# Moving three weight loads and shortening TensorE's last stretch in a fused attention and soft-MoE kernel

## The chip, the cores and the metric

The kernel runs on one core of one Trainium2 chip. The metric is device time in microseconds (us) of one execution, lower is better. A kernel's time is the median of its runs. A profiled execution gives the span, from the first instruction to the last, and a few microseconds lie around it.

## The reference: what is computed

Two layers follow each other. Shapes: batch 4, 8 heads, 768 positions, head size 64; the second layer sees 3072 rows of 512.

```python
# attention over the 6 best of 24 chunks of 32 keys
k_min, k_max = k_chunks.min(axis=3), k_chunks.max(axis=3)
ub = sum(maximum(q * k_min, q * k_max), axis=-1)       # bound per query and chunk
top_chunks = argsort(where(causal, ub, -1e9))[..., -6:]
scores = where(in_top_chunk & causal, q @ k.T / 8, -1e9)
attn_out = softmax(scores) @ v                         # -> x: [3072, 512]

# soft mixture of 8 experts with 4 slots each (32 slots)
logits = x @ phi                                       # phi: [512, 32]
d = softmax(logits, over the 3072 rows)
slot_input = d.T @ x                                   # [32, 512]
slot_out[e] = relu(slot_input[e] @ w1[e]) @ w2[e]      # w1: 512x1024, w2: 1024x512
c = softmax(logits, over the 32 slots)
out = c @ slot_out                                     # [3072, 512], float32
```

All inputs are float32 in memory. The loads turn them into bf16 on the way.

## The kernel before

**Pairs.** The attention works on 16 pairs of heads, four pairs per batch. For a pair i, `load` brings k and q (L146) and `load_v` brings v (L151). `transposes` (TensorE, L211) and `evac_T` (ScalarE, L220) turn k and q; `kmin`, `kmax` and `qsplit` (VectorE) and `ubound` (TensorE) make the bounds; `select` (VectorE's eight-largest operation, L274, and a copy of a flag on GpSimd, L276) finds the chunks; `ns_transposes` turns the resulting mask. `scores` (L303, L313) fills one of six groups of blocks, `expo` (ScalarE, L327) takes the exponential, `mask` (GpSimd, L337) clears the upper triangle of the diagonal blocks, `pv` (L355) multiplies by v, `normalise` (VectorE, L367, L368) divides, and `x_transposes` and `evac_x` turn the result for the second layer.

**Software pipeline.** All of this is written out by hand in one order; each engine executes its instructions in that order. In the loop, pass i takes the scores of pair i, the value product of pair i-1, the normalising of pair i-2, the turning of k and q of pair i+2 and the issue of the k and q loads of pair i+4. Every fourth pass also carries a step of the second layer for the batch that is done (`moe_...`): logits, a running maximum, the exponentials for dispatch and combine, and a dispatch product that is added to `si_acc`.

**Loads.** All loads are issued by GpSimd, in program order, on one queue. The loads use eight semaphores in turn, so that a load is not issued before the eighth load ahead of it has landed. The 16 expert matrices (w_sb, 1 MB each as bf16, L139) are `w_sb[0..7]` = w1 of experts 0 to 7 and `w_sb[8..15]` = w2 of experts 0 to 7. `load_w(0)` stands after the small phi load of the start; the other fifteen are spread over the passes by `wplan`, which says how many weights `weights(i)` issues in pass i: one each in passes 1 (as entry 0), 2, 3, 4, 5, 7, 8, 9, 10, 11, 12, 14 and 15, and two in 13. In passes below 14 they come after the k, q and v issues of the pass.

**The end.** After the loop, the last pair (LAST = 15) is finished: `pv(LAST, [0, 1, 2])`, `pv(LAST, [3])`, transposes and evacuation of pair 14, `pv(LAST, [4, 5])`, logits, transposes of pair 15, column sums of the combine weights (`col_sums`, L710), the last logits. Then come the maxima, the exponentials, the dispatch product (L491) and the experts. `keep(n)` issues n matmuls whose result nobody reads (L698). `experts_in` (L800) multiplies the slots by w1 in two halves of 512 hidden columns, four experts side by side, each in 32 columns of the array. `experts_out` (L838) does so with w2: experts 0 to 3 side by side, then experts 4, 5 and 6 side by side. Expert 7, whose w2 is loaded last, is cut by rows of its matrix into four parts that run side by side (`last_expert_out`, L849). Its four partial sums stand in spare rows of the result, and the combine weights `c_pad` of expert 7 are repeated four times (`spread_c`, L480) so that the last product adds them up. VectorE and ScalarE scale the result into `so_all` (L881 to L885), and the output stage multiplies it by the combine weights, scales it and stores it from the SyncE queue.

## Time and profile before

| what | value |
|---|---|
| median of 3 runs | 162.14 us (161.63 to 162.91) |
| profiled execution, whole | 162.55 us |
| its span | 160.8 us |
| TensorE (PE) matmul busy | 138.5 us, 86% of the span |
| VectorE (DVE) busy | 121.4 us, 75% |
| ScalarE (ACT) busy | 122.8 us, 76% |
| GpSimd (POOL) busy | 102.7 us, 64% |
| bytes moved by the DMA engines | 32.92 MB, mean 205 GB/s |

The page names an engine operation by the program's tiles and the line of the kernel. The line of digits cuts the span into 40 slices of 4.02 us, each digit being the busy share in tenths. The chain of waits follows the work that ended last back in time. In rows of the timeline, the first number is the start in us, the second how long the group lasted; a bracket tells how long the engine had been idle before it and who ended that. In the view of waits, the three numbers are the total in us, how many waits, and the longest. In the view by stretches of time, the columns after the length are the busy time of PE, PE's weight load (PEld), DVE, ACT and POOL, then PE's granted clock, the DMA share and GB/s. In the view of DMA issues, the last number is the time in us from issue to landing.

### The profile page before, as it was taken

Reading aid. Unit: us, or ns where it says so; the run is one execution under the profiler, and the core shown is the slowest. Engines: PE = TensorE matmul, PEld = TensorE weight load, DVE = VectorE, ACT = ScalarE, POOL = GpSimd, SP = SyncE. Lnnn points to the kernel's source line nnn. Section 1 sums busy time; section 2 is a strip of 40 time slices with the busy share of each in tenths; the row PEclk is TensorE's granted clock in tenths of the full one; section 3 lists DMA queues with packets and bytes.
Section 4 is the critical chain, followed back from the end, with each engine's and each line's share of the span. In section 5 each row is a group of like instructions: output and inputs, shape, how many; then the busy total and the mean of one; then the engine's idle time right before and its main releaser. Section 6 shows DMA issues by size and latency. Waiting matters only on the chain.

```text
span 160.8 us, 5896 instructions
## 1 busy us (share of the span) xinstructions
PE 138.5 (86%) x2420; PEld 91.7 (57%) x2420; DVE 121.4 (75%) x433; ACT 122.8 (76%) x169; POOL 102.7 (64%) x203
## 2 busy tenths in 40 slices
PE   7786799999999998999999899969899999987500
PEld 2343366766767686666768576646676854542100
DVE  4465989999999989998988899968862660187620
ACT  3679899999999898999989889968788521166520
POOL 7999577989888696988968986829864800000000
PEclk9999999999999999999999999999999999999965
DMA  3999999999999999999999999999999999329996
GB/s 40 141 120 158 206 197 206 201 182 211 194 210 196 209 200 206 198 182 211 197 210 195 214 191 212 195 207 197 209 203 214 213 217 213 67 71 415 419 419 248
DMA packets 40603, 32.92 MB, mean 205 GB/s; under 512 B 26368, under 2 KB 34816, under 8 KB 40576
## 3 DMA queue, kind: packets, MB, share of 16 engines
q0 software_dynamic: 38416, 26.25, 110.3%
q1 hardware_dynamic: 2160, 6.29, 9.7%
q8 instruction: 19, 0.31, 0.7%
q14 instruction: 8, 0.07, 0.1%
HBM read 52.49 MB, written 6.29 MB: 366 GB/s over the span
## 4 chain that ended last, share of the span: by engine, by line
PE 39%; DMA 23%; ACT 14%; DVE 11%; issue 5%; POOL 4%; DVEq 0%; ACTq 0%; POOLq 0%
DMA k_in<-in_k_dram 15%; ACT e_sb L327 8%; PE sc_ps L303 6%; PE at_ps L355 6%; DMA out_dram<-o_sb 5%; PE sc_ps L313 5%; PE tr_ps L211 4%; PE xT_ps L377 3%; DMA q_in<-in_q_dram 3%; ACT qT L220 3%; DVE mx L274 3%; PE h_ps L800 2%; PE so_ps L838 2%; DVE x_sb L368 2%; PE ub_ps L262 1%
## 5 line engine op out<-in xcount | busy, mean ns | idle before, releaser
L327 ACT ACTIVATE e_sb<-sc_ps 128x1024 bf16<-128x1024 f32 (+1 forms) x96 | 83.1, 917 | 7.1 <-PE sc_ps L313 6.5
L337 POOL TENSOR_SCALAR_AFFINE_SELECT e_sb<-e_sb 128x256 bf16<-128x256 bf16 x96 | 38.1, 414 | 18.5 <-ACT e_sb L327 18.0
L303 PE MATMUL sc_ps<-qT,kT 64*128 64x384 bf16 (+3 forms) x258 | 36.8, 305 | 2.5 <-ACT e_sb L327 1.6
L313 PE MATMUL sc_ps<-nsT,smask 64*128 64x384 bf16 (+2 forms) x294 | 38.1, 284 | 0.1
L355 PE MATMUL at_ps<-v_t,e_sb 128*128 128x65 bf16 x672 | 29.7, 194 | 1.9 <-DVE x_sb L368 1.5
L355 PEld LDWEIGHTS <-e_sb 128*128 128x128 bf16 x672 | 25.6, 98 | 4.1 <-issue 2.6
L274 DVE MAX8 mx<-ub_ps 128x8 f32<-128x8 f32 (+1 forms) x192 | 16.8, 162 | 4.2 <-PE ub_ps L262 4.2
L303 PEld LDWEIGHTS <-kT 64*128 64x128 bf16 x258 | 13.9, 93 | 10.7 <-issue 5.3
L313 PEld LDWEIGHTS <-smask 64*128 64x128 bf16 x294 | 14.9, 94 | 3.9 <-issue 0.6
L151 POOL DMA_DIRECT2D v_t<-in_v_dram x16 | 16.6, 1039 | 0.7 <-PE ns_ps L285 0.5
L229 DVE TENSOR_REDUCE mm<-kT 128x24 bf16<-128x768 bf16 x16 | 15.1, 945 | 2.3 <-ACT kT L220 2.3
L220 ACT COPY kT<-tr_ps 128x768 bf16<-128x768 bf16 x16 | 12.8, 802 | 4.8 <-PE tr_ps L211 4.8
L368 DVE TENSOR_TENSOR x_sb<-at_ps,inv 128x768 bf16<-128x768 f32 (+1 forms) x17 | 15.5, 910 | 0.6
L235 DVE TENSOR_REDUCE mm<-kT 128x24 bf16<-128x768 bf16 x16 | 15.1, 942 | 0.0
L220 ACT COPY qT<-tr_ps 128x768 bf16<-128x768 bf16 x16 | 12.8, 799 | 1.7 <-PE tr_ps L211 1.6
L146 POOL DMA_DIRECT2D k_in<-in_k_dram x16 | 11.7, 733 | 0.9 <-POOLq L930 0.8
L139 POOL DMA_DIRECT2D w_sb<-in_moe_w_dram x16 | 11.4, 711 | 0.9 <-DMA w_sb<-in_moe_w_dram 0.7
L146 POOL DMA_DIRECT2D q_in<-in_q_dram x16 | 11.5, 718 | 0.0
L211 PE MATMUL tr_ps<-ident,k_in 128*64 128x128 bf16 x192 | 8.4, 223 | 2.2 <-DMA k_in<-in_k_dram 1.7
L388 DVE COPY xT_sb<-xT_ps 128x768 bf16<-128x768 bf16 (+1 forms) x15 | 8.0, 536 | 2.6 <-PE xT_ps L377 2.6
L211 PE MATMUL tr_ps<-ident,q_in 128*64 128x128 bf16 x192 | 8.4, 223 | 0.8 <-DMA q_in<-in_q_dram 0.6
L377 PE MATMUL xT_ps<-ident,x_sb 128*128 128x128 bf16 x96 | 8.2, 221 | 0.0
(138 smaller groups left out, 202.7 us busy)
## 6 DMA issues: line engine op xcount, KB each, us to landing
w_sb<-in_moe_w_dram POOLq DMA_DIRECT2D x16, 1024.0 KB, 14.8
out_dram<-o_sb SPq DMA_DIRECT2D x10, 512.0 KB, 4.5
k_in<-in_k_dram POOLq DMA_DIRECT2D x16, 192.0 KB, 10.0
q_in<-in_q_dram POOLq DMA_DIRECT2D x16, 192.0 KB, 10.5
v_t<-in_v_dram POOLq DMA_DIRECT2D x16, 192.0 KB, 10.9
out_dram<-o_sb SPq DMA_DIRECT2D x2, 256.0 KB, 4.3
out_dram<-first SPq DMA_DIRECT2D x2, 128.0 KB, 2.0
out_dram<-first SPq DMA_DIRECT2D x1, 256.0 KB, 2.1
```

Of the source, the lines that this page charges most:

```text
L146: nc.gpsimd.dma_start(out=t, in_=src.rearrange("h (p g) d -> p h (g d)", p=P))
L151: nc.gpsimd.dma_start(out=v_t[i % NV][:, :, :, :D], in_=v[b, 2 * j:2 * j + 2].rearrange("h (g p) d -> p h g d", p=P),)
L211: nc.tensor.matmul(ps[h * 64:(h + 1) * 64, g, :], lhsT=src[:, h, g * D:(g + 1) * D], rhs=ident, is_transpose=True,)
L220: nc.scalar.copy(t.rearrange("d (p g) -> d p g", g=NQT), st.pop((nm + "ps", i)).rearrange("d g p -> d p g"),)
L229: nc.vector.tensor_reduce(mm[:, 0, 0, :], kT, axis=AX.X, op=ALU.min)
L274: nc.vector.max(mx[:, a, :], ub[:, a, :max(8, 4 * t + 4)])
L303: nc.tensor.matmul(ps[:, h, c:c + w], lhsT=kT[r, kg * P:(kg + 1) * P], rhs=qT[r, qs], start=True, stop=False,)
L313: nc.tensor.matmul(ps[:, h, c + (f - t0) * P:c + (l - t0) * P], lhsT=smask[r, x, kg].rearrange("p a b -> p (a b)"), rhs=nsT[r, (f - x * NJ ...
L327: nc.scalar.activation(e[:, :, :w], st.pop(("scps", i, g))[:, :, :w], func=ACT.Exp, scale=scale)
L337: nc.gpsimd.affine_select(out=e[:, :, c:c + P], in_=e[:, :, c:c + P], compare_op=ALU.is_ge, fill=0.0, base=0, pattern=[[0, 2], [1, P]], ch ...
L355: nc.tensor.matmul(o, lhsT=st["e", i, g][:, h, c:c + P], rhs=v_t[i % NV][:, h, kg, :], start=(kg == 0), stop=(kg == t),)
L368: nc.vector.tensor_tensor(st["x", b][:, t0:t1, 2 * j:2 * j + 2, :].rearrange("p t h d -> p h t d"), at[:, :, :, :D], inv.broadcast_to([P, ...
```

## The change

1. `load_w(0)` moves from behind phi to directly behind the q load of pair 1. The v load of pair 0 moves from before the first `select` to behind it.
2. In `wplan`, the weight of pass 5 moves to pass 6, and the weight of pass 10 joins that of pass 11. So w5 is issued after the k, q and v loads of pass 6 instead of before them, and w9 after those of pass 11.
3. In the last pair, the value products of query tiles 3, 4 and 5 share one accumulation and are ordered by the exponential group that feeds them: eight blocks (16 matmuls) before the transposes of pair 14, seven (14 matmuls) after. The column sums move ahead of the transposes of pair 15, and their reciprocal ahead of the last evacuation. The 18 logits of the first three quarters move behind these transposes.
4. The fillers after the dispatch product go from five to two.
5. The w2 matrices are loaded in the order of experts 0, 1, 2, 3, 5, 6, 7, 4. Expert 4 is now the one whose matrix is cut in four for the end. Experts 5, 6 and 7 are cut by rows into four equal shares of six steps, so that 24 matmuls run four side by side. The combine weights get a second repeated block to add the shares up: one of the three exponentials that fill `c_pad` becomes twice as wide, reads overlapping pairs of experts and needs one zeroed spare row in a fixed tile, `lc_sb`. The row of slot sums `zrow` gets one more small copy.

```diff
     load(1, "q")
+    load_w(0)
...
-    load_v(0)
     transposes(1, "q")
     evac_T(1, "q")
     spread_mask(NJ, NQT)
     select(0)
+    load_v(0)
     load_v(1)
...
     make_identity(nc, identf)
-    load_w(0)
     load(4, "k")
...
-    wplan = {0: 1, 2: 1, 3: 1, 4: 1, 5: 1, 7: 1, 8: 1, 9: 1, 10: 1, 11: 1, 12: 1, 13: 2, 14: 1, 15: 1}
+    wplan = {0: 1, 2: 1, 3: 1, 4: 1, 6: 1, 7: 1, 8: 1, 9: 1, 11: 2, 12: 1, 13: 2, 14: 1, 15: 1}
...
-    pv(LAST, [3])
-    at_b = st["at", LAST]
+    at_b = p_sc.tile([P, 2, 512], F32, name="at_ps", tag="sc")
+    def pv_last(blocks, start=False, stop=False):
...
+    pv_last([(3, 0), (3, 1), (3, 2), (4, 1), (4, 2), (4, 4), (5, 2), (5, 4)], start=True)
     x_transposes(LAST - 1)
     evac_x(LAST - 1, copy=nc.scalar.copy)
     normalise(LAST, 0, 3, at_a)
-    pv(LAST, [4, 5])
+    pv_last([(4, 3), (5, 1), (5, 3), (3, 3)])
+    pv_last([(4, 0), (5, 0), (5, 5)], stop=True)
...
-    moe_logits(BL, range(NDG - 1), lg12)
-    x_transposes(LAST, 0, 3)
-    evac_x(LAST, 0, 3, nc.scalar.copy)
-    normalise(LAST, 3, NQT, at_b)
-    x_transposes(LAST, 3, NQT)
-    evac_x(LAST, 3, NQT)
...
     for b in range(BL):
         col_sums(csa[:, b * NQT:(b + 1) * NQT], b)
+    x_transposes(LAST, 0, 3)
+    evac_x(LAST, 0, 3, nc.scalar.copy)
+    normalise(LAST, 3, NQT, at_b)
+    nc.vector.reciprocal(inv_a, csa)
+    x_transposes(LAST, 3, NQT)
+    evac_x(LAST, 3, NQT)
+    moe_logits(BL, range(NDG - 1), lg12)
     moe_logits(BL, range(NDG - 1, NDG), lg12)
...
     keep(2)
     moe_dispatch(BL)
-    keep(5)
+    keep(2)
...
+    def shared_out():
+        parts = [
+            [(5, x) for x in range(6)],
+            [(5, 6), (5, 7), (6, 0), (6, 1), (6, 2), (6, 3)],
+            [(6, 4), (6, 5), (6, 6), (6, 7), (7, 0), (7, 1)],
+            [(7, x) for x in range(2, 8)],
+        ]
+        for n in range(6):
+            for j in range(4):
+                e, fg = parts[j][n]
+                c0 = e * CH - (SPE if j == e - 5 else 0)
+                nc.tensor.matmul(
+                    so_ps[j * CH:(j + 1) * CH, :], lhsT=hT[:, fg, c0:c0 + CH],
+                    rhs=w_sb[E + LATE.index(e)][:, fg * Dm:(fg + 1) * Dm], start=False, stop=(n == 5),
+                )
...
-    experts_out([0], range(4))
+    experts_out(0)
     hidden_T(1)
     slot_sums()
-    experts_out([1], range(4))
-    experts_out([0, 1], [4, 5, 6])
+    experts_out(1)
+    shared_out()
```

More of the change, by code (lines that the diff above doesn't have):

```diff
@@ L99 @@
     c_pad = static.tile([P, NQT, 4, CH], BF16, name="c_pad")
+    lc_sb = static.tile([P, NQT + 1, NS], F32, name="lc_sb")
     si_acc = static.tile([P, NDG + 1, NS], F32, name="si_acc")
@@ L685 @@
     at_a = st["at", LAST]
-    pv(LAST, [3])
-    at_b = st["at", LAST]
+    at_b = p_sc.tile([P, 2, 512], F32, name="at_ps", tag="sc")
+    def pv_last(blocks, start=False, stop=False):
+        for n, (t, kg) in enumerate(blocks):
+            g, c = BLOCK_LAST[(kg, t)]
+            for h in range(2):
+                nc.tensor.matmul(
+                    at_b[:, h, (t - 3) * (D + 1):(t - 2) * (D + 1)],
+                    lhsT=st["e", LAST, g][:, h, c:c + P], rhs=v_t[LAST % NV][:, h, kg, :],
+                    start=(start and n == 0), stop=(stop and n == len(blocks) - 1),
+                )
+    pv_last([(3, 0), (3, 1), (3, 2), (4, 1), (4, 2), (4, 4), (5, 2), (5, 4)], start=True)
     x_transposes(LAST - 1)
@@ L720 @@
     tail = ctx.enter_context(tc.tile_pool(name="tail", bufs=1))
-    inv_a = tail.tile([P, BL * NQT], F32, name="inv_a")
-    nc.vector.reciprocal(inv_a, csa)
     m_old = m_run[(BL + 1) % 2]
```

60 lines of the change are left out of this document (29 added, 31 removed).

## The prediction

> **What bounds the kernel now.** I read the page, then the chain of waits, then the work by stretches of time, then single DMA issues with their time to landing, and last the timeline of the end.
>
> ```profile
> span 160.8 us, 5896 instructions
> DMA  3999999999999999999999999999999999329996
> PE 39%; DMA 23%; ACT 14%; DVE 11%; issue 5%; POOL 4%; DVEq 0%; ACTq 0%; POOLq 0%
> ```
>
> The DMA engines show 9 from the second slice to the 34th (about 4 to 137 us), while they load; the output follows. So there are two candidates for the start of the output stage: the loads, which move without a break, and the chain, most of which is PE. Both have to be followed to their meeting point.
>
> ```profile
> 118.63 0.77 POOL L139 DMA_DIRECT2D w_sb<-in_moe_w_dram  x1
> w_sb<-in_moe_w_dram POOLq DMA_DIRECT2D x1, 1024.0 KB, 21.5
> 140.21 0.28 PE L849 MATMUL so_last<-w_sb,hT_pad 128*32 128x256 bf16 x1
> 140.67 0.39 PE L849 MATMUL so_last<-w_sb,hT_pad 128*32 128x256 bf16 x6
> 140.89 0.49 DVE so_part L881
> 141.48 0.50 DVE so_all L883
> ```
>
> They meet here. The last weight is issued at 118.6 and lands 21.5 later, at 140.1; its first matmul starts at 140.21, on the landing. The other arm, PE's shared experts, lets DVE start so_part at 140.89, done at 141.38. Had PE been free, the eight so_last matmuls would end about 0.4 after the landing (six take 0.39 at 140.67), at 140.6, and so_all waits for so_part until 141.38. So today the compute arm is the later one, and the loads have only about 0.75 us of slack. A saving on one arm alone is worth little: compute alone at most 0.75, loads alone nothing.
>
> **The compute arm, part by part.**
>
> ```profile
> PE tr_ps L211 <- DMA k_in<-in_k_dram: 1.7, 2, 1.3
> 57.90 11.24 DMA k_in<-in_k_dram
> 93.29 12.66 DMA k_in<-in_k_dram
> ```
>
> *Two weights behind late k loads.* The chain passes through two k loads, those of pairs 10 and 15, and PE stood still for the two for 1.7 us in all (0.4 and 1.3). Each has a weight ahead of it in the queue. The change sends the k, q and v of pair 10 before w5, and those of pair 15 before w9, so each k lands earlier by one weight. A weight takes about 4.9 us (1,048,576 B at the 214 GB/s of the stretch from 18 to 22 us, shown below), far over 0.4 and 1.3. Both waits go; the loads behind the moved weight keep their place in the sum of bytes. What is late next: the chain is back on PE right after each wait, so I count the whole 1.7.
>
> ```profile
> 125.71 0.86 PE L355 MATMUL at_ps<-v_t,e_sb 128*128 128x65 bf16 x22
> 126.76 0.64 PE lgt_ps L400 x16
> 131.37 1.17 PE L698 MATMUL h_ps<-w_sb,ident 128*128 128x480 bf16 x5
> 131.63 0.35 DVE L773 TENSOR_TENSOR siT_pad<-si_acc,si_ps 128x64 bf16<-128x64 f32 x2 [0.38 <-PE si_ps L495]
> 132.48 2.77 PE L800 MATMUL h_ps<-w_sb,siT_pad 128*32 128x512 bf16 x48
> 136.57 0.86 PE so_ps L838 x16
> 138.09 2.31 PE so_ps L838 x34
> ```
>
> *Last pair.* After the transposes of pair 14, PE has 22 value matmuls in 0.86 (0.039 each) ahead of the second normalise. Eight of them now stand before the transposes, where DVE's normalise of pair 14 has PE waiting anyway, and 14 remain: 0.3 less. Against this, 18 logits (0.04 each by the row of 16, so 0.7) move behind the last transposes, into the time in which PE waited for the evacuation. If they overrun it, the 0.3 is gone. Between 0 and 0.3 I take 0.2. The column sums move ahead, into a wait for DVE; the reciprocal that reads them moves off the last logits into the same wait. I cost both at nothing.
>
> *Dispatch.* Five filler matmuls last from 131.37 to 132.54, and the experts start at 132.48, though siT_pad is written by 131.98. Three fillers fewer (0.2 each) take 0.6 away, but the experts still need siT_pad: start at 132.03, 0.45 less.
>
> *Experts.* With four experts side by side, 16 matmuls, four rounds, take 0.86: 0.215 a round. The shared three ran three side by side, 24 matmuls in eight rounds; now the same 24 run in six. Two rounds, 0.43. The row of 34 holds the second sixteen of the first four experts and most of the 24, and PE waits for nothing in it, so fewer rounds are less time.
>
> Sum of the compute arm: 1.7 + 0.2 + 0.45 + 0.43 = 2.8 us.
>
> *Costs at nothing.* In each batch one of three exponentials reads 192 elements instead of 96. An ACT row with 192 elements takes 0.33:
>
> ```profile
> 130.29 0.33 ACT L750 ACTIVATE d_sb<-lgt_ps 128x192 bf16<-128x192 f32 x1 [2.21 <-PE lgt_ps L741]
> ```
>
> so at most 0.33 is added per batch and 1.0 over the three inside the pairs, where ACT is nearly full; I take 0 because ACT's waits for PE in those pairs cover it, and keep the end for the range. At the end the ACT is idle until the first relu. The extra zrow copy is on a POOL that is empty by then.
>
> **The load arm.** Bytes do not change; only stretches in which the queue runs slowly can be won.
>
> ```profile
> 2.00:6.00 4.00, 3.41 (x21) 1.19 (x19) 0.95 (x13) 0.69 (x2) 3.83 (x10) 1.00 0.88 118
> 6.00:9.00 3.00, 2.48 (x40) 1.35 (x41) 2.38 (x4) 2.88 (x5) 3.00 (x5) 1.00 1.03 134
> 9.00:12.50 3.50, 3.14 (x42) 1.79 (x39) 2.67 (x16) 2.22 (x4) 3.32 (x6) 1.00 1.00 113
> 12.50:18.00 5.50, 3.37 (x50) 1.86 (x47) 3.80 (x19) 5.50 (x7) 4.71 (x11) 1.00 1.86 170
> 18.00:22.00 4.00, 3.56 (x69) 2.33 (x69) 3.35 (x18) 3.25 (x5) 2.21 (x5) 1.00 1.08 214
> 24.00:130.00 106.00, 100.53 (x1958) 72.62 (x1956) 92.51 (x327) 94.32 (x127) 82.72 (x162) 1.00 1.35 202
> ```
>
> The last column is GB/s. From 6 to 12.5 us the small loads crawl at 134 and 113, mean 123; later small loads alone reach 170, the first weight alone 214, the mixture 202. With w0 right behind the second q, the weight moves in that stretch. At 214 it takes 4.9 us; in 4.9 us the stretch moves 600 KB of small loads today, and these now follow at 170 (3.5 us) to 202 (3.0). The queue gains 4.9 − 3.5 = 1.4 to 4.9 − 3.0 = 1.9. If the weight crawls at 123 too, it gains nothing; with 214 for all, 2.1. I take 1.65, the middle of the two, since the rows nearest to it are this same weight and these same loads a few us later. The last weight then lands at 138.5.
>
> *What the moved weight pushes back.*
>
> ```profile
> q_in<-in_q_dram POOLq DMA_DIRECT2D x1, 192.0 KB, 4.3
> 4.75 0.74 POOL L146 DMA_DIRECT2D q_in<-in_q_dram  x1
> 12.81 0.72 POOL L139 DMA_DIRECT2D w_sb<-in_moe_w_dram  x1
> w_sb<-in_moe_w_dram POOLq DMA_DIRECT2D x1, 1024.0 KB, 10.6
> 13.52 0.72 POOL L146 DMA_DIRECT2D k_in<-in_k_dram  x1
> k_in<-in_k_dram POOLq DMA_DIRECT2D x1, 192.0 KB, 10.8
> 14.96 1.49 POOL L337 TENSOR_SCALAR_AFFINE_SELECT e_sb<-e_sb 128x256 bf16<-128x256 bf16 x4
> 15.95 0.53 PE L211 MATMUL tr_ps<-ident,k_in 128*64 128x128 bf16 x12
> 17.18 0.23 POOL L276 CAST ns_t<-mx 128x12 bf16<-128x12 f32 x1 [0.73 <-DVE mx L274]
> 21.31 0.55 PE L355 MATMUL at_ps<-v_t,e_sb 128*128 128x65 bf16 x12
> ```
>
> The second q lands at 4.75 + 4.3 = 9.1. Behind it w0 lands by 14.0, and a k or q takes about 1 us (w0 lands at 23.4, the k after it at 24.3): k of pair 2 at 15.0, needed at 15.95; its q at 16.0; v of pair 0, four loads and its own two us later, at 20, needed at 21.31. All in time, with about 1 us. On POOL the weight's issue (0.72) moves ahead of two masks and the loads of pairs 2 and 3, and the v issue (about 1 us) from before the first selection to behind it, so by that selection POOL has lost nothing. One new wait stands there: the loads take eight semaphores in turn, each load waits for the landing of the eighth before it, and in the changed order the q of pair 4 waits for the landing of pair 2's k. Behind it in POOL's queue stand four masks (1.49) and the flag copy that PE's next mask transposes need, at 17.18 today. 15.0 + 0.72 + 1.49 = 17.2: just in time. Up to 0.2 is possible; I take 0.
>
> **Where the arms meet.** Compute gains 2.8; the loads allow 0.75 + 1.65 = 2.4. The smaller counts: 2.4, so PE waits some 0.4 for the last weight. The output stage is not touched. The profiled execution took 162.55 us, span 160.8 plus 1.75 around it: 162.55 − 2.4 = 160.15, span 158.4. The execution lies 0.4 above the median of the runs, 162.14, which gives **159.7**.
>
> **The rivals.**
>
> *The first weight fills nothing.* Then the loads allow only today's 0.75: 162.14 − 0.75 = 161.4. For it: the slow stretch is one of small loads only, and if it belongs to them they are as slow behind the weight. The Trainium skill, DMA: Bandwidth & Descriptors, section Bandwidth, Measured, says it so: "Batch DMAs to ≥1 MiB for ≥75% of peak", with small transfers dominated by their descriptors; by it the 600 KB would still take 4.9 us and the gain be 0. Against it: 192 KB loads move at 170 from 12.5 us on, and the k behind w0 lands 0.9 us after it, over 200 GB/s; in that place the trace does not agree with the rule. 0.20.
>
> *The k waits only change their name.* PE is fed no faster because ACT or DVE, both nearly full in the pairs, end the next wait: compute gains 1.1 instead of 2.8, 162.14 − 1.1 = 161.0. Against it: the chain returns to PE after both waits. 0.12.
>
> *Slower: the start stalls.* If w0 crawls too, everything behind it is late. Each us past 14.0 at which w0 lands delays pair 2's k, the slot, the masks, the flag copy and so PE by one. At 113 GB/s w0 takes 9.3, lands at 18.4, 4.4 late; against 2.8 gained this is 1.6 lost: 163.7. It decides from 2.8 late, 16.8, which is 136 GB/s, about what the stretch moves today. Against it: packets of a weight ran at 214 beside the same work six us later. 0.08.
>
> **How the numbers follow.** Forecast 159.7 has 0.55: with loads at 1.4 to 2.1 and compute at 2.5 to 2.8 it spans 159.3 to 160.1. A better case, in which the last weight's straggling engines end closer together too (from 136 to 140.2 few of the 16 are busy) and compute keeps 2.8 to 3.5, 158.6 to 159.3, has 0.05. The range 158.8 to 161.4 leaves the slow start, half of the better case and the edge of the first rival out. A measurement tells about 1%, 1.6 us, from no change: faster takes the forecast, the better case and some tenth of the middle rivals, 0.65; same 0.30; slower, the tail of the slow start, 0.05.
>
> **What would show it.** In the profile after: no wait of PE for k near 69 and 106 us; w0 landing near 14 and 200 GB/s or more in the stretch from 8 to 13; pair 2's k before PE asks; the last weight landing near 138.5 with its first matmul right on it; shared experts in six rounds of 0.215; the experts' start right behind siT_pad. I am wrong if the GB/s of 6 to 13 stays near 123, if POOL's wait for the slot ends after 15 us, or if another wait replaces those for k.

## The result and the profile after

| | median us | runs | profiled execution | its span |
|---|---|---|---|---|
| before | 161.88 | 161.37 to 162.91 | 162.55 | 160.8 |
| after | 164.37 | 164.01 to 165.15 | 164.12 | 162.4 |

The changed kernel is slower: the ratio is 1.0145, with an interval of 1.0098 to 1.0192. The kernel before has one run more here than in the table ahead of the prediction, so its median is 161.88 instead of 162.14. The forecast was 159.7 us and its range ended at 161.4. In the kernel after, line numbers are 2 to 26 higher than in the kernel before; the tiles have the same names.

The page of the kernel after: its span, its DMA row and the shares of the chain.

```profile
span 162.4 us, 5892 instructions
DMA  3999999999999999999999999999999999329996
PE 30%; DMA 21%; DVE 19%; ACT 14%; POOL 6%; issue 5%; ACTq 0%; DVEq 0%; POOLq 0%; SPq 0%
```

PE's share of the chain fell from 39 to 30%. The shares alone do not say what took its place (that of DMA fell too, from 23 to 21%). The meeting point of the two arms, the loads and PE's own work, does: it is the last weight that ends last. In the view of DMA issues (last number: us from issue to landing)

```profile
w_sb<-in_moe_w_dram POOLq DMA_DIRECT2D x1, 1024.0 KB, 21.7
```

and in the timeline of GpSimd, PE and DVE:

```profile
119.89 0.77 POOL L141 DMA_DIRECT2D w_sb<-in_moe_w_dram  x1
...
139.44 1.47 PE L865 MATMUL so_ps<-w_sb,hT_pad 128*32 128x512 bf16 x24
140.97 0.48 DVE L907 TENSOR_SCALAR so_part<-so_ps,zinv 128x256 f32<-128x256 f32 x1 [2.17 <-PE so_ps L865]
141.67 0.40 PE L875 MATMUL so_last<-w_sb,hT_pad 128*32 128x256 bf16 x8 [0.76 <-DMA w_sb<-in_moe_w_dram]
142.65 0.60 PE L918 MATMUL oh_ps<-so_all,cT_all 128*128 128x256 bf16 x4 [0.37 <-DVE so_all L909]
```

The last weight lands at 119.89 + 21.7 = 141.6. Before it was 140.2, and the forecast had 138.5. PE now stands 0.76 us for it, which it did not do before. But PE's own arm is no earlier either: so_part is read at 140.97, against 140.89 before. The output begins at 142.65, which is 0.63 later than before (142.02), and the output stage then takes 19.77 us to the end of the span instead of 18.79. That makes 0.63 + 0.98 = 1.6 us, the difference of the two spans. (The profiles of two kernels below, e11 and e14, were taken in a disturbed execution and are not read.) There are three things to explain: where PE's saving went, why the last weight is late, and why a stage that the change does not touch is longer.

**PE's saving was made, and lost at the start.** The view of waits of the kernel after (us in all, times, longest):

```profile
PE tr_ps L215 <- DMA k_in<-in_k_dram: 0.8, 2, 0.6
```

The timeline of its dispatch:

```profile
132.70 0.35 DVE L782 TENSOR_TENSOR siT_pad<-si_acc,si_ps 128x64 bf16<-128x64 f32 x2 [0.31 <-PE si_ps L497]
132.98 2.77 PE L810 MATMUL h_ps<-w_sb,siT_pad 128*32 128x512 bf16 x48
```

The waits for k of pairs 10 and 15 are gone; 0.6 of the 0.8 us that is left is a new one at 16.92. The experts start 0.28 us after siT_pad begins to be written (before: 0.85). The 24 shared matmuls take 1.47 in one row. Measured between the same instructions, PE is 2.7 us late at k of pair 4 (30.02 against 27.29), 1.3 late at k of pair 15 (107.25 against 105.99), and 0.1 late at so_part. So passes (1.5), last pair (0.2), dispatch (0.57) and experts (0.42) returned some 2.65 us, and the start had taken 2.7.

**The start.** The view by stretches of the kernel after (last column GB/s, before it the DMA share and PE's granted clock):

```profile
6.00:9.00 3.00, 2.94 (x31) 1.13 (x29) 2.31 (x4) 2.97 (x5) 2.99 (x6) 1.00 1.02 150
9.00:12.50 3.50, 3.11 (x44) 1.91 (x46) 2.39 (x16) 2.22 (x3) 2.66 (x5) 1.00 0.96 151
12.50:18.00 5.50, 3.50 (x53) 1.78 (x46) 3.64 (x18) 4.88 (x6) 3.18 (x6) 1.00 1.19 197
18.00:22.00 4.00, 2.12 (x29) 1.30 (x29) 2.66 (x6) 2.10 (x4) 3.50 (x9) 0.82 2.11 168
```

Up to 18 us each stretch but the one from 2 to 6 moves more than before (150, 151 and 197 GB/s against 134, 113 and 170), together about 0.3 MB. But from 18 to 22 us, where the weight ran at 214 before, the small loads now move at 168, which gives more than half of it back.

The issues of the q of pair 1 and of the first weight, with the time to landing:

```profile
q_in<-in_q_dram POOLq DMA_DIRECT2D x1, 192.0 KB, 4.5
w_sb<-in_moe_w_dram POOLq DMA_DIRECT2D x1, 1024.0 KB, 10.4
```

GpSimd's and then PE's timeline around the k of pair 2:

```profile
16.44 0.72 POOL L148 DMA_DIRECT2D k_in<-in_k_dram  x1 [1.99 <-PE ub_ps L266]
17.41 0.71 POOL L148 DMA_DIRECT2D q_in<-in_q_dram  x1 [0.26 <-issue]
18.14 1.49 POOL L341 TENSOR_SCALAR_AFFINE_SELECT e_sb<-e_sb 128x256 bf16<-128x256 bf16 x4
19.60 0.23 POOL L280 CAST ns_t<-mx 128x12 bf16<-128x12 f32 x1
...
16.92 0.53 PE L215 MATMUL tr_ps<-ident,k_in 128*64 128x128 bf16 x12 [0.59 <-DMA k_in<-in_k_dram]
19.88 0.34 PE L289 MATMUL ns_ps<-ident,ns_t 128*128 128x128 bf16 x3 [2.00 <-POOL ns_t L280]
```

The q of pair 1 lands at 4.75 + 4.5 = 9.25 and the weight at 5.49 + 10.4 = 15.9, so the weight takes 6.6 us, 159 GB/s, where the forecast gave it 4.9 at 214. The k of pair 2, behind it, lands at 16.88 instead of 11.42; PE uses it at once, having waited 0.59. GpSimd's issues of pair 4 come at 16.44 and 17.41. The profile names PE for the first of the two waits, but counted by the eight semaphores the eighth load ahead of that k is the first weight (landed 15.90) and the eighth ahead of that q is the k of pair 2 (16.88). Both issues follow these landings by 0.53 to 0.54 us, and so they do in other kernels in which the landings fall elsewhere (in e15, below, 15.84 on 15.30 and 16.78 on 16.25); so it is the semaphores, not PE. Behind them stand the masks, at 18.14 instead of 14.96, and the flag copy, at 19.60 instead of 17.18. PE waits 2.00 us for the flag copy.

Two consequences follow at once, in the views by stretches of the kernel after:

```profile
20.54:23.95 3.41, 3.41 (x45) 2.07 (x39) 2.22 (x12) 2.74 (x3) 1.61 (x3) 0.50 1.86 176
24.00:26.00 2.00, 2.00 (x44) 1.41 (x40) 1.97 (x10) 1.74 (x3) 1.87 (x5) 1.00 1.30 98
26.00:28.00 2.00, 2.00 (x43) 1.44 (x37) 1.69 (x4) 2.00 (x3) 2.00 (x4) 1.00 0.94 154
```

After PE's wait its granted clock is 0.50 for 3.41 us. And since the next loads are issued when the passes reach them, the second weight is issued at 24.07 instead of 21.64; the queue of loads runs low. From 24 to 28 us it moves 98 and 154 GB/s, 126 in the mean against 205 before: 0.31 MB less. Up to 24 us the changed kernel had moved 0.1 MB more than the kernel before, so by 28 us it is 0.2 MB behind, 1.0 us of loading at 200 GB/s. Of the 1.46 us by which the last weight is late, this is the larger part. From 60 to 66 us another 0.16 MB is lost (178 GB/s against 205). Kernels with the new weight plan and no early weight are below 205 there too (e1 and e5 below: 191 and 187).

**The output stage.** The first two stores of the output in SyncE's timeline, before and then after:

```profile
142.90 0.87 SPq L898 DMA_DIRECT2D out_dram<-first  x2
```

```profile
143.53 1.47 SPq L924 DMA_DIRECT2D out_dram<-first  x2
```

The two issues take 0.87 us before and 1.47 after; it is the second of them that grew, from 0.44 to 1.05. The DMA queues in just this stretch of the kernel after (143.53 to 145.00; packets, MB, share):

```profile
q1 hardware_dynamic: 138, 0.13, 25.2%
q8 instruction: 1, 0.02, 4.0%
```

One instruction packet runs in it. The page counts 19 of them with 0.31 MB, so 16 KB each; this one takes 0.94 us. In the kernel before, the packet runs from 142.52 to 143.40 and is nearly over when the second issue begins, at 143.33. I call it the code packet; whether it is the cause is tested below.

### The profile page after: what moved, and what is told of

It is laid out like the page before. It is cut to its first block, busy times and chain, and to the rows that moved or that the text cites. A ratio compares the mean times of both kernels' runs of the same rounds, so it can differ in the third digit from the quotient of the medians.

```text
span 162.4 us, 5892 instructions
## 1 busy us (share of the span) xinstructions
PE 139.4 (86%) x2417; PEld 92.0 (57%) x2417; DVE 122.8 (76%) x434; ACT 123.2 (76%) x169; POOL 103.3 (64%) x204
## 4 chain that ended last, share of the span: by engine, by line
PE 30%; DMA 21%; DVE 19%; ACT 14%; POOL 6%; issue 5%; ACTq 0%; DVEq 0%; POOLq 0%; SPq 0%
DMA w_sb<-in_moe_w_dram 13%; ACT e_sb L331 8%; PE sc_ps L307 6%; DMA out_dram<-o_sb 5%; PE tr_ps L215 5%; PE sc_ps L317 5%; PE at_ps L359 4%; ACT qT L224 4%; DVE mx L278 3%; DVE x_sb L372 2%; POOL e_sb L341 2%; PE xT_ps L381 2%; DMA k_in<-in_k_dram 2%; PE ub_ps L266 2%; DVE o_sb L898 2%
## 5 line engine op out<-in xcount | busy, mean ns | idle before, releaser
L307 PE MATMUL sc_ps<-qT,kT 64*128 64x384 bf16 (+3 forms) x258 | 37.3, 309 | 2.6 <-ACT e_sb L331 1.7
L317 PE MATMUL sc_ps<-nsT,smask 64*128 64x384 bf16 (+2 forms) x294 | 38.7, 288 | 0.1
L359 PE MATMUL at_ps<-v_t,e_sb 128*128 128x65 bf16 x642 | 28.4, 194 | 1.5 <-DVE x_sb L372 1.0
L359 PEld LDWEIGHTS <-e_sb 128*128 128x128 bf16 x642 | 24.6, 98 | 3.7 <-issue 2.3
L278 DVE MAX8 mx<-ub_ps 128x8 f32<-128x8 f32 (+1 forms) x192 | 16.8, 162 | 4.0 <-PE ub_ps L266 3.9
L215 PE MATMUL tr_ps<-ident,k_in 128*64 128x128 bf16 x192 | 9.0, 234 | 0.8 <-DMA k_in<-in_k_dram 0.8
L253 DVE TENSOR_SCALAR qpn<-qT 128x768 bf16<-128x768 bf16 x15 | 9.2, 613 | 0.0
```

Source lines behind the costliest of these rows:

```text
L215: nc.tensor.matmul(ps[h * 64:(h + 1) * 64, g, :], lhsT=src[:, h, g * D:(g + 1) * D], rhs=ident, is_transpose=True,)
L278: nc.vector.max(mx[:, a, :], ub[:, a, :max(8, 4 * t + 4)])
L307: nc.tensor.matmul(ps[:, h, c:c + w], lhsT=kT[r, kg * P:(kg + 1) * P], rhs=qT[r, qs], start=True, stop=False,)
L317: nc.tensor.matmul(ps[:, h, c + (f - t0) * P:c + (l - t0) * P], lhsT=smask[r, x, kg].rearrange("p a b -> p (a b)"), rhs=nsT[r, (f - x * NJ ...
L359: nc.tensor.matmul(o, lhsT=st["e", i, g][:, h, c:c + P], rhs=v_t[i % NV][:, h, kg, :], start=(kg == 0), stop=(kg == t),)
```

## The experiments

Ratios are against the kernel before on the same chip; the intervals are of 95%. The kernel before took 161.8 to 162.3 us in these comparisons. Positions in a kernel (us from the start of the span) are from its one profiled execution.

### Undoing the first weight, and doing it alone

The first kernel is the changed one with the loads of the first weight and of the first v where they were. The second is the kernel before with only these two loads moved.

```diff
 e1: after                      e2: before
     load(1, "q")                    load(1, "q")
-    load_w(0)                  +    load_w(0)
...
     make_identity(nc, identf)       make_identity(nc, identf)
+    load_w(0)                  -    load_w(0)
```

Expected of the first:

> The changed kernel with the first weight and the v load of pair 0 back where they were before; the new weight plan and the new end stay. Theory A (the early first weight alone costs the time: it lands 2 us later than worked out, holds GpSimd at the slot of the q load of pair 4, and TensorE starts late): the start runs as before the change, TensorE's arm ends about 2.6 us earlier than before (so_part near 138.3), the last weight lands near 140.1 as before and is what the end waits for: 161.0 to 161.4. Theory B (the weight plan or the new end costs the time): stays at 163.5 or more.

Expected of the second:

> The kernel before with only the first weight and the v load of pair 0 moved. Theory A: TensorE late by 2.5 to 2.8 us after the start, the loads behind it issued late, the last weight near 141.6 or later, so_part at 141.5 to 143: 163.5 to 165. Theory B: 161.5 to 162.5.

Measured: 163.42 us, ratio 1.0079 (1.0049 to 1.0108) without the early weight; 164.74 us, ratio 1.0140 (1.0069 to 1.0211) with it alone. The early weight alone costs 2.3 us by the ratio (1.1 to 3.4), as expected, and has the whole mechanism of the start, with waits of 0.90 for the k and 2.01 for the flag copy (PE, second kernel):

```profile
16.94 0.53 PE L212 MATMUL tr_ps<-ident,k_in 128*64 128x128 bf16 x12 [0.90 <-DMA k_in<-in_k_dram]
19.91 0.50 PE L286 MATMUL ns_ps<-ident,ns_t 128*128 128x128 bf16 x3 [2.01 <-POOL ns_t L277]
```

Some 0.65 us of this is not of the start: the second kernel's output stage takes 19.44 us and its second store issue 1.13, because the code packet falls there too, although the end is that of the kernel before. Taking the early weight back leaves 1.3 us of loss by the ratio, where 161.0 to 161.4 had been expected: the rest of the change, which saves PE 2.85 us, is a loss of its own. The timeline of PE's and SyncE's end of the first kernel (e1),

```profile
140.28 0.40 PE L875 MATMUL so_last<-w_sb,hT_pad 128*32 128x256 bf16 x8 [2.29 <-DMA w_sb<-in_moe_w_dram]
...
142.25 1.92 SPq L924 DMA_DIRECT2D out_dram<-first  x2
```

and a stretch of it:

```profile
140.60:144.01 3.41, 3.21 (x21) 1.41 (x13) 2.11 (x4) 2.30 (x5) 0.00 (x0) 0.50 0.14 42
```

PE's arm is 2.85 us earlier (so_part at 138.04), the last weight lands at 140.24 as before, and PE waits 2.29 us for it. The output starts at 141.27, 0.75 earlier than before, the slack that the prediction had read off. Then it is lost: PE's granted clock is halved as the output starts, the two store issues take 1.92 us, and the stage lasts 20.32 us instead of 18.79.

### Moving the loads of pair 4, and the place of the weight

Third kernel: the changed one with the loads of pair 4 behind the masks. Fourth: as the third, and the first weight between the k and the q of pair 2.

```diff
 e3 and e4
     make_identity(nc, identf)
-    load(4, "k")
-    load(4, "q")
...
     mask(0, 4)
+    load(4, "k")
+    load(4, "q")
 e4 only
     load(1, "q")
-    load_w(0)
...
     load(2, "k")
+    load_w(0)
     load(2, "q")
```

> The changed kernel, with the k and q loads of pair 4 issued behind the masks of groups 0 to 4 of pair 0 and the flag copy of pair 1, so that GpSimd meets the slot wait after them. Theory A1 (the slot wait on GpSimd is what makes TensorE late): the flag copy stands at 17.2 to 17.6 again, TensorE is late by 1.0 or less from pair 2 on, the queue does not run dry between 24 and 30 us, the last weight lands at 138.8 to 139.5: 160.2 to 161.0. Theory A2 (the k, q and v that land late behind the weight do it themselves): TensorE still late by 2 or more, 163.5 or more.

> As the run with the late k and q of pair 4, and the first weight issued one load later, between the k and the q of pair 2. Theory A1: the k of pair 2 lands by 12.5, TensorE is late by 0.5 or less, the last weight lands at 138.6 to 139.3: 159.7 to 160.5. Theory A2: the q of pair 2 and the v of pair 0 land as late as in the changed kernel (17.9 and 21.5), TensorE late by 1 or more: 161.5 or more.

Measured: 163.41 us, 1.0060 (1.0028 to 1.0093), and 163.93 us, 1.0110 (1.0067 to 1.0154). In the third kernel (e3) neither theory's figures came: PE is 1.5 us later than before at k of pair 4 (28.77). The wait of GpSimd is gone. From the use of the k of pair 2 to that of pair 4, PE takes 11.18 us, against 13.10 in the changed kernel and 11.34 before: so that part of the mechanism stands, at 1.8 us with the half clock behind it. But the first weight landed later still (16.57), the output stage is 19.85 us long, and the last weight is where it was before (140.34). PE's wait for the k of pair 2 is 1.6 us here, and the granted clock falls behind it as well (view of waits, then a stretch):

```profile
PE tr_ps L215 <- DMA k_in<-in_k_dram: 1.9, 2, 1.6
```

```profile
18.00:22.00 4.00, 3.86 (x43) 2.01 (x38) 2.87 (x6) 3.09 (x4) 2.50 (x4) 0.57 2.11 169
```

In the fourth (e4) the k of pair 2 lands at 11.11 again, yet the weight itself, landing at 18.22, is no faster, the last weight lands at 141.36 and the stage is 20.16. PE is 1.2 us late at k of pair 4 (28.52), with the q of pair 2 at 18.62 and the v of pair 0 at 22.11: this is the second theory, A2. Placing the weight one load later gained nothing that can be told here.

### Is it the wait for the last weight, the code packet, or the loads?

Four kernels. The plan alone is the kernel before with the new `wplan`. The next three are the changed kernel without the early first weight, and: with 20 filler multiplications in PE's wait; with the six fillers of the dispatch cut into 48 narrow ones; with one weight less to load (the second matrix of expert 5, whose products then use the tile of expert 3, so that part of the output differs).

```diff
 e5: before                     e7: fill
-    wplan = {..., 5: 1, ..., 10: 1, 11: 1, ...}
+    wplan = {..., 6: 1, ..., 11: 2, ...}
...
     shared_out()
     nc.vector.tensor_scalar_mul(so_part, so_ps[:, HD:], zinv)
+    fill = p_tp.tile([P, 512], F32, name="fill_ps", tag="tp")
+    for _ in range(20):
+        nc.tensor.matmul(fill[:, :256], lhsT=ident, rhs=w_sb[E][:, :256], start=True, stop=True)
 e8: split, in keep(n)
-            nc.tensor.matmul(h_ps[0][:, 1, CH:], lhsT=ident, rhs=w_sb[0][:, CH:512], ...)
+            for c in range(CH, 512, 60):
+                nc.tensor.matmul(h_ps[0][:, 1, c:c + 60], lhsT=ident, rhs=w_sb[0][:, c:c + 60], ...)
 e9: one weight less
     def load_w(i):
+        if i == 12:
+            return
...
+        if i == 12:
+            w_sb.append(w_sb[11])
+            continue
```

The plan alone:

> The kernel before with only the new weight plan (two weights behind the late k loads); first weight and last pair as before. Theory L (the loads set the end at about 140.2 us whatever TensorE saves, and TensorE's wait for the last weight lengthens the output stage from 18.8 to 19.4 to 20.3 us): k waits fall by 1.2 to 1.7 us, TensorE then waits 0.5 to 1.3 us for the last weight, output starts at 141.2 to 141.6 instead of 142.0, time 162.2 to 163.3, no better than before. Theory P (the prediction's: the output stage stays at 18.8): time 161.4 to 161.8.

The filler in the wait:

> The changed kernel with the first weight put back, and 20 filler multiplications of 128x256 between the shared weights' products and the last weight's, so that TensorE isn't idle in its 2.29 us wait; they also move the code packet of TensorE 40 instructions forward. Theory L (idle TensorE and code packet make the output stage 1.5 us longer): granted clock 1.0 from 140 to 144, the packet ends ahead of the second store's issue, which takes 0.4 us instead of 1.5; output starts at 141.2 and the stage takes 18.8 to 19.3; time 161.2 to 162.0. If neither matters: 163.4 as without the filler, or more by what the filler overruns.

The split fillers:

> The changed kernel with the first weight put back, and the 6 filler multiplications of 480 columns at the dispatch written as 48 of 60: the same columns, 42 multiplications (with their weight loads 84 instructions) more ahead of the output stage, no filler in the wait for the last weight. This moves the code packet alone. If the packet is what holds the second store's issue: that issue takes 0.4 us instead of 1.5, stage 19.2 to 19.7 (the half clock at its start stays), time 162.3 to 162.8. If the half clock alone makes the stage long: 163.4, and the issue still 1.0 to 1.5.

One weight less:

> The changed kernel with the first weight put back and the load of one late weight left out (the second matrix of expert 5; its products are taken from the tile of expert 3's, so this part of the output is another). 4.9 us of loads less: last weight at 135.4 instead of 140.2. Theory L: TensorE no longer waits for it, output starts at 139.0 to 139.4, time 158.8 to 161.0 by whether the stage takes 18.8 or 20.3. If the loads are not the bound: output at 141.3 and 163.4 as with all loads.

Measured: plan alone 161.91 us, 0.9973 (0.9943 to 1.0004); filler 162.40 us, 1.0020 (0.9999 to 1.0041); split 162.08 us, 1.0006 (0.9973 to 1.0039); one weight less 161.25 us, 0.9934 (0.9897 to 0.9970). All four medians lie outside what was expected of the time, by 0.2 to 0.4 us: plan and split below, filler and one weight less above. The ends of these four in their timelines, PE and SyncE: the plan alone,

```profile
140.77 0.40 PE L849 MATMUL so_last<-w_sb,hT_pad 128*32 128x256 bf16 x8 [1.33 <-DMA w_sb<-in_moe_w_dram]
...
142.63 0.85 SPq L898 DMA_DIRECT2D out_dram<-first  x2
```

the filler, then its stretch after the last weight's landing,

```profile
138.05 2.36 PE L910 MATMUL fill_ps<-w_sb,ident 128*128 128x256 bf16 x20
...
142.21 0.84 SPq L927 DMA_DIRECT2D out_dram<-first  x2
```

```profile
140.60:144.01 3.41, 2.77 (x31) 1.46 (x20) 2.77 (x6) 2.62 (x6) 0.00 (x0) 1.00 0.23 76
```

the split fillers and a stretch of the same length,

```profile
143.82 0.84 SPq L926 DMA_DIRECT2D out_dram<-first  x2
```

```profile
143.21:146.62 3.41, 3.19 (x15) 1.64 (x13) 2.67 (x5) 2.79 (x5) 0.00 (x0) 0.50 0.52 187
```

and one weight less:

```profile
138.24 0.39 PE L879 MATMUL so_last<-w_sb,hT_pad 128*32 128x256 bf16 x8
...
139.60 0.76 PE L922 MATMUL oh_ps<-so_all,cT_all 128*128 128x256 bf16 x4 [0.20 <-DVE so_all L913]
140.48 1.67 SPq L928 DMA_DIRECT2D out_dram<-first  x2
```

The readings:
- *The loads are the bound.* With 4.9 us of loading less, PE no longer waits for the last weight, the output starts at 139.60 instead of 141.27, and the time falls by about 2.3 us (ratio 1.0079 to 0.9934). In the plan alone the two k waits go as forecast, and 1.33 us of the saving come back as a wait for the last weight: 0.2 us gained, not told apart from nothing. This fell below the range expected for it (162.2 to 163.3), because the stage stayed at 18.77.
- *The code packet lengthens the stage.* With narrow fillers, 84 more instructions on TensorE ahead of the end, the packet comes 3 us before the output; the store issues are back at 0.84, and the ratio falls from 1.0079 to 1.0006, 1.2 us. With 40 more instructions in the wait itself the issues are at 0.84 too. Where the end is the changed one and nothing is shifted, as with one weight less, they take 1.67. The traces of all kernels here, those below too, say more. In all nine in which the packet is still running when the second issue begins (before, after, e1 to e4, e6, e9, e16), this issue ends 0.36 to 0.38 us after the packet does (after: packet to 144.63, issue to 145.00; e1: 143.79 and 144.17); in the others it takes 0.42 to 0.43. The first issue takes 0.37 to 0.38 even inside the packet. And the stage less its second issue is nearly a constant: 18.31 to 18.35 us with the end of the kernel before, 18.72 to 18.76 with the changed end at the full clock. So of the 0.98 us in the kernel after, 0.61 are the packet's and some 0.4 belong to the changed end.
- *The half clock carries little.* Filling PE's wait holds the granted clock at 1.00 and the stage takes 19.16 us; with the split fillers the clock falls to 0.50 as the output starts and the stage takes 19.23. (This profiled execution, 163.88 us, lies above the kernel's median because its last weight landed at 141.91.) By the constant above the half clock adds 0.1 (18.81 and 18.82 in e8 and e1). The kernel with the full clock is not shown to be the faster one.

### The end alone, and the mending of the start

Four more: the kernel before with only the new end of TensorE's work; the changed kernel with split fillers; this with the second weight issued right behind the third pair's v; and this with the loads of pair 4 late as well.

```diff
 e6: after, first weight and wplan as before
 e10, e11, e12: after, keep(n) split as in e8
 e11, e12
     load_v(2)
+    weights(0)
...
-        if i == 1:
-            weights(0)
 e12: pair 4's loads behind mask(0, 4), as in e3
```

> The kernel before with only the shorter chain of TensorE (last pair, dispatch, experts, and the few instructions around them); first weight and weight plan as before. Chain alone: compute 1.1 us shorter, but the last weight still lands at 140.2, so output starts at 141.2 to 141.8. Theory L with the code packet (this end has 6 TensorE instructions less, so the packet comes 1.0 us behind the start of the output instead of 0.1 to 0.5, onto the second store's issue): that issue takes 1.0 us or more, stage 19.5 to 20.3, time 162.4 to 163.4, slower than the plan alone (161.9). If the packet has nothing to do with this end: issue 0.4 us, time 161.5 to 162.0.

> The changed kernel with the 6 filler multiplications at the dispatch written as 48 of 60 columns, nothing else (first weight early). Theory L: the code packet leaves the first stores, the second issue takes 0.4 us instead of 1.05: 0.6 to 1.3 us less than the changed kernel's 164.4, 163.1 to 163.8; the last weight still lands at 141.4 to 142.0, and this is then the whole rest against before. If the early first weight costs by another way than the late last weight: 164.4.

> As the one with the split fillers, and the second weight's load issued right behind the third pair's v (about 21.5 instead of 24.1 us), so that the queue of loads doesn't run dry at 24 to 28 us (98 and 154 GB/s there, 0.30 MB less than at 200 GB/s: 1.5 us of loading). Theory A (the late start costs by that hole): last weight lands at 140.0 to 140.4 instead of 141.6; TensorE's own work is then the bound, output starts at 142.0 to 142.3, time 162.3 to 163.2. If the last weight is late for another reason (loads slower all along): it lands at 141.4 or later and the time stays that of the split fillers alone.

> As the one before, and the loads of pair 4 issued behind the masks, so that TensorE loses 1.2 us less at the start. Theory A: last weight 139.7 to 140.4, shared part's read at 139.7 to 139.9, output starts at 141.0 to 141.4, stage 18.8 to 19.3, time 161.3 to 162.2: the early first weight brings nothing against before even with its damage undone. A gain of the prediction's size (load arm 1.65 us shorter) would show as a last weight at 138.6 and a time of 160.5 or less.

Measured: end alone 162.78 us, 1.0044 (1.0018 to 1.0070); changed kernel with split fillers 163.69 us, 1.0086 (1.0044 to 1.0128); with the second weight early 164.77 us, 1.0155 (1.0111 to 1.0200); with pair 4 late too 162.26 us, 1.0006 (0.9973 to 1.0038). SyncE's first stores of the end alone, then of the changed kernel with split fillers:

```profile
143.69 1.75 SPq L924 DMA_DIRECT2D out_dram<-first  x2
```

```profile
143.65 0.84 SPq L926 DMA_DIRECT2D out_dram<-first  x2
```

The end alone saves PE about 1.2 us and is 0.7 us slower than before by the ratio: with 6 TensorE instructions less, its code packet falls on the first stores (1.75 us for the two issues; this profiled execution, 164.60 us, lies above the median). In the changed kernel, moving the packet takes 0.6 us from the stage (19.77 to 19.16); the ratio falls from 1.0145 to 1.0086, though the intervals meet.

The second weight early did not do what was expected: alone its median is higher still, though the intervals meet. Together with the later loads of pair 4 the loss is gone. A stretch of that kernel (e12), and its end on DVE and PE:

```profile
24.00:26.00 2.00, 2.00 (x41) 1.47 (x38) 1.97 (x6) 2.00 (x4) 2.00 (x5) 1.00 1.33 207
```

```profile
138.95 0.48 DVE L908 TENSOR_SCALAR so_part<-so_ps,zinv 128x256 f32<-128x256 f32 x1 [2.17 <-PE so_ps L866]
139.30 0.40 PE L876 MATMUL so_last<-w_sb,hT_pad 128*32 128x256 bf16 x8 [0.41 <-DMA w_sb<-in_moe_w_dram]
```

The hole from 24 us on is filled and the last weight lands at 139.26, in the profiled execution, 161.16 us. Its ten runs lie between 161.16 and 164.06, and the ratio is the same as that of e8 (1.0006), which has the same split fillers and no early weight. An early first weight with all its damage mended brings nothing that can be measured.

### TensorE's clock at the start

Three kernels fill PE's two waits around the second pair's k with idle multiplications: the last of those above (3 and 2 of them), the one with the second weight early (3 and 9), and the changed one with split fillers (3 and 9).

```diff
+    warm(3)
     transposes(2, "k")
...
     expo(0, 5)
+    warm(2)          # 9 in the other two
     ns_transposes(1)
```

> As the one with pair 4 late, the second weight early and the fillers split, and 3 and 2 idle multiplications of 128x512 in TensorE's two waits (0.60 and 0.46 us) around the second pair's k, so that it isn't idle there. That kernel's ten times spread from 161.2 to 164.1, and its profile, of the fastest of them, shows no half clock at the start. Theory H (the half clock at the start, drawn in some executions only, makes the spread): median 161.2 to 161.8, none over 162.6. If the clock isn't the cause: 162.3 and the same spread.

> As the one with the second weight early and the fillers split (pair 4 early), and 3 and 9 idle multiplications in the two waits of TensorE (0.6 and 2.0 us) around the second pair's k. Theory H: granted clock 1.0 at 18 to 26 us, fourth pair's k used at 22.6 to 23.2 instead of 23.8, time 163.0 to 163.8 instead of 164.8. Without H: 164.8.

> The changed kernel with the fillers split, and the same 3 and 9 idle multiplications; the second weight at its place. Theory H: no half clock at 20.9, k of pairs 3 and on 0.5 to 0.8 us earlier, second weight issued as much earlier, last weight at 140.9 to 141.4 instead of 141.7, time 162.7 to 163.3 instead of 163.7. Without H: 163.7.

Measured: 162.13 us, 1.0008 (0.9981 to 1.0035); 163.60 us, 1.0076 (1.0046 to 1.0106); 162.90 us, 1.0070 (1.0038 to 1.0102). The same stretch of the changed kernel with split fillers, without and with the idle multiplications:

```profile
22.00:26.00 4.00, 4.00 (x67) 2.91 (x65) 3.09 (x17) 3.14 (x5) 2.86 (x6) 0.71 1.35 120
```

```profile
22.00:26.00 4.00, 4.00 (x81) 2.77 (x80) 3.48 (x16) 3.88 (x6) 3.44 (x8) 1.00 1.26 107
```

The clock stays at 1.00, k of pair 3 is used 0.70 us earlier (22.27 against 22.97), the last weight lands 0.74 earlier (141.00 against 141.74). Not all of this is the clock's. In this execution the first weight landed 0.47 earlier (15.30 against 15.77), and PE's use of the flag copy is already 0.43 earlier (19.41 against 19.84). From there to k of pair 4, PE takes 9.29 us instead of 10.11; these 0.82 are the clock's, as far as one execution of each can show. The medians of the second and third lie where they were expected. Against the kernel before on the same chip, the ratio of the second falls from 1.0155 to 1.0076, that of the third only from 1.0086 to 1.0070, not told apart from nothing. In the first the upper tail is gone (161.2 to 162.7) but the median stayed: there the clock explains the spread at most, and the expectation of 161.2 to 161.8 was missed.

### A version meant to beat both

The kernel before with its own end, the new weight plan and the mended start.

```diff
 e16: before + load_w(0) early + new wplan + e12's two moves + warm(3), warm(2)
```

> The kernel before with its own end (so the code packet stays off the first stores), the new weight plan, and the mended start: first weight early, pair 4's loads behind the masks, second weight behind the third pair's v, 3 and 2 idle multiplications around the second pair's k. With both arms about 0.7 us shorter (last weight at 139.3 to 140.3, shared part's read at 139.9 to 140.4), output starts at 141.1 to 141.6 and the stage takes 18.8: 161.2 to 161.8, up to 0.5 % under before. If the early first weight brings the loads nothing: as the plan alone, 161.9.

Measured: 162.94 us, 1.0038 (1.0009 to 1.0066), slower than the kernel before, and than the plan alone; both expectations were missed. PE's first use of pair 2's k, in the kernel with the same start and the changed end (e13):

```profile
16.67 0.53 PE L215 MATMUL tr_ps<-ident,k_in 128*64 128x128 bf16 x12
```

In this one (e16):

```profile
18.54 0.53 PE L212 MATMUL tr_ps<-ident,k_in 128*64 128x128 bf16 x12 [1.52 <-DMA k_in<-in_k_dram]
```

The same loads in the same order landed at other times: the first weight at 15.65 and the k of pair 2 at 16.61 in the one execution, at 16.24 and 18.49 in the other, and with the weight ahead of that k this comes out on PE: 1.9 us. The rate from 9 to 12.5 us does not explain it. It was 202 and 153 GB/s in these two, but 151 in the changed kernel, where that k landed at 16.88. Why the k came 2.25 us behind the weight here is not shown. This profiled execution, 163.76 us, lies above the median, so how much of the median this explains stays open too; and 0.3 us of it is the code packet, which lengthens the second store issue to 0.73 even with the end of the kernel before. Before, that k landed at 11.42 for a use at 15.95, 4.5 us ahead. No complete version here is shown to be faster than the kernel before; the plan alone comes nearest.

## Why the prediction was wrong, step by step

- **Two arms with 0.75 us of slack on the loads**: right. Without the early weight PE saves 2.85 us and the output starts 0.75 earlier, not more; with the plan alone PE waits 1.33 us for the last weight.
- **The compute arm, 2.8 us**: right, about 2.65. The k waits gave 1.5 of 1.7, the last pair 0.2 of 0.2, dispatch 0.57 of 0.45, the experts 0.42 of 0.43. The rival in which the k waits only change their name is out; the wider exponentials cost nothing that shows.
- **The first weight at 214 GB/s in the slow stretch, gain 1.65 us**: this step failed first. It ran at 159, so it took 6.6 us instead of 4.9 (landed 15.9, not 14.0). The small loads, put where the weight had run at 214, moved at 168, and the loads of pair 4 landed only 0.7 us earlier instead of 1.65. The row taken as nearest was of the same weight six us later; the row of the place itself, 134 and 113 GB/s, was nearer. With the damage mended, the rival in which the first weight fills nothing comes nearest: e12 gains nothing against e8. The Trainium skill, DMA: Bandwidth & Descriptors, section Bandwidth, Measured, blames small transfers for low rates, those under 64 KB above all; the loads here are of 192 KB. The trace agrees only in part: the small loads are slower than the weight at 18 to 22 us (168 against 214), but a 1 MB weight at the start ran at 159 GB/s too, so the rate belongs to these first us and not to the size of the loads alone.
- **Landing times "all in time, with about 1 us"; the slot wait "just in time"**: wrong by the same error. The k of pair 2 came 0.9 us after its old use, and the slot wait, at 17.41, set back masks and flag copy by 2.4 to 3.2 us. The mechanism was named, its price was taken as 0. With the half clock that follows it, it was 1.8 us (13.10 against 11.34 from the k of pair 2 to that of pair 4, and 11.18 where the slot wait is moved away, in e3). The sum 15.0 + 0.72 + 1.49 also left out the 0.53 us from a landing to the issue that waits for it.
- **The slower rival**, the start stalls if the weight crawls: this is what happened, at a chance of 0.08. Its price was too low. It let PE be late by the 1.9 us that the weight is past 14.0, and it weighed this against PE's saving alone. It missed that PE's wait halves the granted clock, and above all that a late PE issues the next loads late, so that the load arm, which had little slack, loses 1.5 us too. By its own account it decided from 16.8 us; the weight landed at 15.9 and it had already decided.
- **"The output stage is not touched"**: wrong. Its code is the same, but it took 0.98 us more. Of this the code packet carries 0.61, the growth of the second store issue; the kernels that moved it (e8, e10) show it. The prediction counted instructions saved on TensorE, not where the next packet of instructions falls.

The sum: the output was to start 2.4 us earlier and started 0.6 later, 3.0; the stage 1.0; and the profiled executions lie 0.4 above (before) and 0.25 below (after) their medians, 0.65. Together this is the 4.7 us between 159.7 and 164.4.

What stays open: why the second weight issued early, alone, did not help; why the k of pair 2 lands so differently behind the early weight; and 0.4 us by which the output stage stays longer (19.2 against 18.8) in every profile with the changed end, the packet out of its way.

## What to carry to other kernels

Where two arms meet with little slack, price a change by what it does to the arm that has less: here a late PE also made the loads late, and PE's own 2.65 us could never be worth more than 0.75. A large load put ahead of small ones takes their cover; if their landings vary from one execution to the next, the variation then reaches the result. After any edit that moves the end, above all one that adds or removes instructions, look at where the instruction packets fall beside the first stores.

## What the runs showed of the hardware

- A 16 KB instruction packet takes 0.9 to 1.4 us here, and SyncE's second store issue, where the packet was still running, ended 0.36 to 0.38 us after it in nine profiles: it took 0.44 to 1.50 us instead of 0.42. The first store issue was not lengthened, even inside the packet (before, e16). Adding 40 to 84 TensorE instructions moved the packet ahead of the stores. The Trainium skill, Runtime: NRT & Kernel Launch, section Instruction fetch mechanics, has the blocks of 16 KiB and says that their fetch is mostly hidden; the trace shows that another engine's store issue can pay for it.
- PE's granted clock went to 0.50 for 3.41 us after waits of 1.6 (e3) and 2.00 us (after) at the start and of 2.29 us (e1) at the end; after waits of 1.52 us at the start (e16) and of 0.76 (after), 1.33 (e5) and even 2.12 us (e4) at the end it did not. So the length of one wait does not decide it alone. The Trainium skill, TensorE: Matmul & The Clock Gate, section Part 1: The HAM clock gate, puts the limit at an idle window of about 3.4 us; here shorter waits were sometimes enough.
- The loads between 9 and 12.5 us ran at 151 to 206 GB/s in the kernels with the first weight right behind the q of pair 1, and at 113 to 142 in those without it; from 30 to 60 us all of them move 192 to 200.
